# Rotary attention and softplus feed-forward on one core: the first head pair rotated through PSUM and placed by engines, the second on GpSimd, weight group 0 converted in mid loop

## Chip, cores and metric

The kernel runs on one core of one Trainium2 chip. The metric is the device time of one execution in microseconds (us). Time before the change: 745.19 us, the median of 3 runs (744.81 to 746.87).

## What is computed

Attention with rotary position embedding over 4 batches of 8 heads, 576 positions of 64 values each, and behind it a feed-forward of 2304 tokens with a softplus between two matrix products. Inputs and result are float32, the feed-forward's weights come as float64.

```python
def _attn_ref(q, k, v):                       # 4 x 8 x 576 x 64
    def rotate(x):
        x1, x2 = (x[..., :half], x[..., half:])
        return np.concatenate([x1 * cos - x2 * sin, x1 * sin + x2 * cos], axis=-1)
    q_rot, k_rot = (rotate(q), rotate(k))
    scores = scale * np.matmul(q_rot, k_rot.transpose(0, 1, 3, 2))
    scores = scores - np.max(scores, axis=-1, keepdims=True)
    attn = np.exp(scores)
    attn = attn / (np.sum(attn, axis=-1, keepdims=True) + 1e-09)
    return np.matmul(attn, v)

def _moe_ref(x, w_in, w_out):                 # 2304 x 512, 512 x 2048, 2048 x 512
    h = x @ w_in
    g = np.maximum(h, 0.0) + np.log1p(np.exp(-np.abs(h)))
    return g @ w_out
```

## The kernel before

Every matrix product is made exact enough by splitting an operand into a rounded high part and the rest (low part), both in the matmul's 32-bit format, and adding the products.

**Attention** is one loop over slots `s`; slot `s` belongs to head `s // 5` and chunk `s % 5` of 128 positions, 160 slots in all, followed by a tail. A head passes through three passes on TensorE (PE), all written into the same slot sequence. `p1` (L356) computes scores of the slot's chunk, and VectorE (DVE) takes their maximum (L358). `p2`, nine slots later (L390), computes the scores again, transposed and with the maximum subtracted as two more rows of the stacked query; ScalarE (ACT) takes the exponential twice (L396, L397) and DVE makes its low part (L404, L407). `pv`, twelve slots behind `p1` (L425), multiplies with the values. So the slots 0 to 8 hold `p1` alone, and from slot 12 on a slot holds all three.

Between `p1` and `p2` of a head lies its **shift**: GpSimd (POOL) splits the five maxima (`shift1`, tile `shl`), PE transposes them (`shift2`, L373, in slot 5h + 6 for head h), ACT rounds the result (`shr`, L375) and a DMA from ACT's queue writes it into the stacked query (`shift3`, L379, `qs<-shr`). `p2` of the head starts three slots behind the transpose and waits for that DMA.

**Rotation** goes by pairs of heads. The arrays of a pair (`raw`, one for q and one for k, 576 KB each) hold both halves in two orders, so that a rotation is: multiply with the cosine table, multiply with the sine table, add, round to the high part, subtract to the low part (`rope_steps`, L303 and L297/L300; `tab` is the table). Four DMAs per head (`stack`, L335 to L338) then place the parts into the stacked operands `qs` and `ks`, of which there are four each. Pairs 2 and on are rotated a pair ahead in the loop. Of the first pairs, pair 0 is rotated by DVE and POOL and ACT ahead of the loop, and pair 1 in slots 0 to 5.

**The feed-forward** (L203, L239) starts behind slot 168 and goes over 16 groups of the weights. A group's float64 words are turned into float32, split and stored by `conv_w`. Group 0 is loaded ahead of the loop and converted in slots 1 to 9 by ACT and DVE; group 1 is loaded in slots 92 to 134 and converted in slots 141 to 156 (`early`, `STEPS`), with its add (L146) and its low part (L151) on POOL; the others follow from slot 152 on.

**What sets the order.** A scheduler lays out the instructions; those wrapped in `pin` keep the order in which they are written, those in `chain` follow one another on their queue. Each engine, and SyncE's (SP's) DMA queue, works its instructions in that order. A warm-up of 64 matmuls on zeros (L283) fills PE until the first operands are there.

The few lines to which the steps of the prediction point:

```python
e0, e1, e2, e3 = "VVAV" if p == 0 else "VPAV" if p + i == 2 else "PPAP" if p == 1 else "PPPP"
...
if n < LAG and n % 2:
    sp = ps_v.tile([128, 2, 512], F32, tag="pv", name="sp1")
else:
    sp = ps_1.tile([128, 2, 512], F32, tag="s1", name="sp1")
```

The letters say which engine (V for DVE, P for POOL, A for ACT) does which step of a rotation. The scores of `p1` lie in a single buffer, and in slots 0 to 8 in two.

Of the kernel before, what the change touches and what calls it, by code (L numbers as in the profile page):

```python
# [30 lines left out]
FC = 2  # L31
SEG = 4
# [8 lines left out]
WARM = 64  # L41
# [11 lines left out]
def rope_attention_softplus_moe(  # L53
# [210 lines left out]
    def attention(es, es_r, es_s, tail):  # L264
# [16 lines left out]
        wp = ps_2.tile([128, 2, 512], F32, tag="s2", name="wp")  # L281
# [23 lines left out]
        def rope_steps(p):  # L305
            for i in range(2):
# [3 lines left out]
                e0, e1, e2, e3 = "VVAV" if p == 0 else "VPAV" if p + i == 2 else "PPAP" if p == 1 else "PPPP"  # L310
                yield tt(a, a, tab[:, 0, :], ALU.mult, e0)
                yield tt(b, b, tab[:, 1, :], ALU.mult, e1)
                yield tt(a, a, b, ALU.add, e0)
                yield rnd(hi[:, :S], a, e2)
                yield tt(lo[:, :S], a, b, ALU.subtract, e3)
                if i:
                    rnd(hi[:, S:], hi[:, 512:S].bitcast(F32), e2)
                    rnd(lo[:, S:], lo[:, 512:S].bitcast(F32), e2)
# [23 lines left out]
        def p1(n):
# [5 lines left out]
            if n < LAG and n % 2:  # L348
# [340 lines left out]
```

## Time and profile before

| | |
|---|---|
| median of 3 runs | 745.19 us |
| the profiled execution | 744.38 us |
| its span, first to last instruction | 742.5 us |
| PE busy | 717.1 us (97%) |
| DVE, ACT, POOL busy | 501.8, 384.3, 314.3 us |
| mean granted TensorE clock | 0.986 |
| first matmul on scores | 23.11 us |
| transposes of the shifts of heads 0, 1, 2 | 32.32, 43.40, 53.89 us |

Busy times are sums over the whole span, and the stages differ: up to some 50 us the engines wait for one another, from there to some 290 us the attention loop runs in an even beat, and behind it the feed-forward fills PE. Times in the rows are counted from the span's start; 1.88 us of the profiled execution lie outside its span.

### The profile page before, as it was taken

The page shows a single profiled execution, that of the slowest core. Times are in us where ns is not written, and L with a number is a line of the kernel's source. Part 1 is how long each engine was busy: PE and PEld are TensorE (multiplying, and loading weights), DVE is VectorE, ACT ScalarE, POOL GpSimd, SP SyncE. Part 2 cuts the span into 40 slices and gives each one's busy share as a digit, 9 for nine tenths or more (in the row PEclk, how much of TensorE's full clock was granted, in tenths as well). Part 3 has the DMA queues.
Part 4 walks back from the last instruction along what each step waited for, and adds up shares of the span by engine and source line. Part 5 has one row for each costly group of instructions (what it writes and reads, how often), then busy time and mean ns, then how long its engine had stood idle before and what let it go on. Part 6 is the DMA issues. An engine that isn't in the chain of part 4 may idle for free.

```text
span 742.5 us, 11791 instructions
## 1 busy us (share of the span) xinstructions
PE 717.1 (97%) x4288; PEld 671.2 (90%) x4288; DVE 501.8 (68%) x784; ACT 384.3 (52%) x718; POOL 314.3 (42%) x384
## 2 busy tenths in 40 slices
PE   6599999999999999999999999999999999999997
PEld 6489999999999999998999989899998989999996
DVE  7688888888788888877989989453443343344333
ACT  2267777777777777875666666232222222222221
POOL 5269999898899988884000000370400000000000
PEclk9589999999999999999999999999999999999999
DMA  7948887889898977702333333160010010001001
GB/s 235 240 133 203 202 202 199 201 219 213 216 248 215 242 186 180 198 21 85 123 114 114 129 102 115 35 203 22 22 43 0 1 44 1 0 1 43 0 1 44
DMA packets 46219, 89.05 MB, mean 120 GB/s; under 512 B 6768, under 2 KB 16304, under 8 KB 46160
## 3 DMA queue, kind: packets, MB, share of 16 engines
q1 hardware_dynamic: 43184, 83.41, 42.5%
q10 hardware_dynamic: 2976, 4.88, 1.8%
q8 instruction: 34, 0.56, 0.3%
q14 instruction: 25, 0.20, 0.1%
HBM read 48.64 MB, written 7.23 MB: 75 GB/s over the span
## 4 chain that ended last, share of the span: by engine, by line
PE 88%; DVE 5%; DMA 4%; ACT 2%; issue 1%; SPq 0%; ACTq 0%; DVEq 0%
PE hp L203 26%; PE pv L425 14%; PE oa L239 13%; PE ob L239 13%; PE sp L390 11%; PE sp L356 10%; DMA qs<-shr 2%; DVE raw L303 2%; DMA tab<-cs 1%; DMA ks<-raw 1%; DVE mx L358 1%; ACT ph L396 0%; ACT raw L297 0%; ACT sp L397 0%; DVE g L223 0%
## 5 line engine op out<-in xcount | busy, mean ns | idle before, releaser
L203 PE MATMUL hp<-x,wh 128*128 128x384 f32 x768 | 196.3, 336 | 1.2 <-DVE m L218 1.2
L358 DVE TENSOR_REDUCE mx<-sp 128x1 f32<-128x576 f32 x160 | 120.9, 755 | 55.0 <-PE sp L356 45.0
L215 ACT ACTIVATE e<-e 128x384 f32<-128x384 f32 x96 | 50.4, 525 | 198.4 <-DVE e L213 193.7
L203 PEld LDWEIGHTS hp<-x,wh 128*128 128x128 f32 x768 | 140.6, 188 | 9.8 <-DVE m L218 1.6
L356 PE MATMUL sp<-ks,qs 128*128 128x288 f32 x640 | 117.5, 308 | 13.4 <-DMA ks<-raw 9.4
L396 ACT ACTIVATE ph<-sp 128x576 fp32r<-128x576 f32 x160 | 103.8, 649 | 50.7 <-PE sp L390 50.4
L203 PE MATMUL hp<-x,wl 128*128 128x384 f32 x384 | 129.3, 337 | 0.0
L390 PE MATMUL sp<-qs,ks 128*128 128x288 f32 x640 | 114.5, 300 | 2.6 <-DVE ph L407 1.2
L356 PEld LDWEIGHTS sp<-ks,qs 128*128 128x128 f32 x640 | 96.6, 196 | 17.4 <-issue 9.6
L425 PE MATMUL pv<-ph,vs 128*64 128x288 f32 (+1 forms) x640 | 110.7, 295 | 0.0
L213 DVE TENSOR_SCALAR e<-hp 128x384 int32<-128x384 int32 x96 | 53.2, 555 | 75.4 <-PE hp L203 75.4
L397 ACT ACTIVATE sp<-sp 128x576 f32<-128x576 f32 x160 | 102.8, 642 | 0.0
L404 DVE TENSOR_TENSOR pl<-sp,ph 128x576 fp32r<-128x576 f32 x128 | 96.6, 755 | 5.6 <-ACT sp L397 4.2
L390 PEld LDWEIGHTS sp<-qs,ks 128*128 128x128 f32 x640 | 93.6, 190 | 5.5 <-DMA qs<-shr 2.4
L239 PE MATMUL oa<-wh,g 128*128 128x512 f32 x288 | 97.7, 393 | 0.0
L239 PE MATMUL ob<-wh,g 128*128 128x512 f32 x288 | 97.3, 393 | 0.0
L223 DVE TENSOR_TENSOR g<-m,g 128x384 fp32r<-128x384 f32 x96 | 56.4, 588 | 46.8 <-ACT g L220 46.8
L425 PEld LDWEIGHTS pv<-ph,vs 128*64 128x64 f32 (+1 forms) x640 | 86.7, 161 | 0.1
L303 POOL TENSOR_TENSOR raw<-raw,tab 128x576 f32<-128x576 f32 x58 | 82.6, 1446 | 9.2 <-DMA raw<-qk 9.1
L303 POOL TENSOR_TENSOR raw<-raw 128x576 f32<-128x576 f32 (+1 forms) x56 | 81.0, 1446 | 5.2 <-ACT raw L297 3.0
L218 DVE SCALAR_TENSOR_TENSOR m<-hp,e 128x384 f32<-128x384 f32 x96 | 53.5, 557 | 42.9 <-ACT e L215 41.4
L220 ACT CAST g<-m 128x384 fp32r<-128x384 f32 x96 | 49.3, 513 | 48.9 <-DVE m L218 46.0
(75 smaller groups left out, 884.9 us busy)
## 6 DMA issues: line engine op xcount, KB each, us to landing
raw<-qk SPq DMA_DIRECT2D x32, 576.0 KB
wraw<-w SPq DMA_DIRECT2D x30, 512.0 KB
ks<-raw SPq DMA_DIRECT2D x32, 320.0 KB
qs<-raw SPq DMA_DIRECT2D x32, 288.0 KB
ks<-raw SPq DMA_DIRECT2D x32, 160.0 KB
vf<-v SPq DMA_DIRECT2D x32, 160.0 KB
qs<-raw SPq DMA_DIRECT2D x32, 144.0 KB
x<-xt SPq DMA_DIRECT2D x16, 144.0 KB
```

The costliest lines, as they stand in the source:

```text
L203: pin(nc.tensor.matmul(out=hp, lhsT=a[f][:, c * 128:(c + 1) * 128], rhs=piece(j, c)[:, b, :], start=(i == 0), stop=(i == 11),))
L218: pin(nc.vector.scalar_tensor_tensor(out=m, in0=hp, scalar=0.0, in1=e, op0=ALU.max, op1=ALU.add))
L223: pin(nc.vector.tensor_tensor(out=g[:, 1, :], in0=m, in1=g[:, 0, :].bitcast(F32), op=ALU.subtract))
L239: pin(nc.tensor.matmul(out=po, lhsT=g[:, s, t * 128:(t + 1) * 128], rhs=b[f][:, 512:1024], start=(first and i == 0), stop=(last and i == 2),))
L303: pin((nc.vector if e == "V" else nc.gpsimd).tensor_tensor(out=out, in0=in0, in1=in1, op=op))
L356: pin(nc.tensor.matmul(out=sp[:, j, :HS], lhsT=q[:, i, cq], rhs=k[:, 0, ck], start=(i == 0), stop=(i == 1)))
L358: pin(nc.vector.tensor_reduce(out=mx_t[h][:, c:c + 1], in_=sp[:, :, :HS], axis=AX.XY, op=ALU.max, negate=True))
L390: pin(nc.tensor.matmul(out=sp[:, i, :HS], lhsT=k[:, j, ck], rhs=q[:, j, hs], start=(j == 0), stop=(j == 1)))
L396: pin(nc.scalar.activation(out=ph, in_=sp, func=AF.Exp, scale=D ** -0.5))
L397: pin(nc.scalar.activation(out=sp, in_=sp, func=AF.Exp, scale=D ** -0.5))
L404: pin(nc.vector.tensor_tensor(out=pl, in0=sp[:, :, :HS], in1=ph.bitcast(F32), op=ALU.subtract))
L425: pin(nc.tensor.matmul(out=pv[rows, i, :HS], lhsT=lhs, rhs=rhs[:, i, :], start=(c == 0 and j == 0), stop=(c == 4 and j == len(terms) - 1)))
```

## The change

- **Arrival.** The first q array comes in two halves on SP's queue, the table in two halves on ACT's queue, ahead of ACT's table load. The k array of pair 0, both arrays of pair 1 and both of pair 2 follow at once on SP. Nothing of weight group 0 is loaded here. The warm-up has 54 matmuls and lies in another PSUM buffer.
- **Pair 0** (`place_pair0`). ACT copies the table into PSUM (`ct`, `st`). DVE rotates q into a PSUM tile (`sq`) and k into `ct`. ACT and DVE then write high and low parts from PSUM straight into `qs` and `ks` of heads 0 and 1, across partitions where needed. The eight placing DMAs of this pair fall away.
- **Pair 1** (`rope_pair1`). All multiplications, sums and differences are POOL's, and are issued ahead of the loop and in slots 1, 2, 3 and 5; ACT rounds the high parts. Its placing DMAs follow in slots 2 (queries) and 5 (keys).
- **Pair 2** is rotated wholly by POOL (`PPPP`), as all later pairs are; before, its q array was `VPAV`.
- **Group 0** of the weights is loaded in slots 40 to 82 and converted in slots 96 to 111, in the steps of group 1, so with two adds and two subtractions on POOL.
- The memsets of two stacked queries go to DVE, those of the third and of the values' ones to POOL.

```diff
-WARM = 64
+WARM = 54
+W0 = 40
-STEPS = {141: (0,), 143: (0,), 147: (0, 1), ..., 156: (1,)}
+STEPS = {0: (0,), 2: (0,), 6: (0, 1), 7: (0,), 8: (0, 1), 10: (0,), 11: (1,), 12: (1,), 13: (1,), 15: (1,)}
+BASE = (96, 141)
...
-        wp = ps_2.tile([128, 2, 512], F32, tag="s2", name="wp")
+        wp = ps_1.tile([128, 2, 512], F32, tag="s1", name="wp")
...
+        def rope_pair1():
...
+            (qh, ql, qa, qb), (kh, kl, ka, kb) = parts
+            tt(qa, qa, tab[:, 0, :], ALU.mult, "P")
+            tt(qb, qb, tab[:, 1, :], ALU.mult, "P")
+            tt(qa, qa, qb, ALU.add, "P")
+            yield
+            rnd(qh[:, :S], qa, "A")
+            tt(ka, ka, tab[:, 0, :], ALU.mult, "P")
+            yield
+            tt(ql[:, :S], qa, qb, ALU.subtract, "P")
+            tt(kb, kb, tab[:, 1, :], ALU.mult, "P")
+            tt(ka, ka, kb, ALU.add, "P")
+            yield
+            rnd(kh[:, :S], ka, "A")
+            rnd(kh[:, S:], kh[:, 512:S].bitcast(F32), "A")
+            yield
+            tt(kl[:, :S], ka, kb, ALU.subtract, "P")
+            rnd(kl[:, S:], kl[:, 512:S].bitcast(F32), "P")
+            yield
...
+        def place_pair0():
+            ct, st = (ps_2.tile([128, 2, 512], F32, tag="s2", name=k) for k in ("ct", "st"))
+            sq = ps_v.tile([128, 2, 512], F32, tag="pv", name="sq")[:, :, :HS]
+            ct, st = ct[:, :, :HS], st[:, :, :HS]
+            pin(nc.scalar.copy(out=ct, in_=halves(tab[:, 0, :])))
+            pin(nc.scalar.copy(out=st, in_=halves(tab[:, 1, :])))
...
+            tt(qa, qa, tab[:, 0, :], ALU.mult, "V")
+            tt(qb, qb, tab[:, 1, :], ALU.mult, "V")
+            tt(sq, halves(qa), halves(qb), ALU.add, "V")
+            rnd(halves(q0[L, 0, :S]), sq[L], "A")
+            rnd(halves(q0[H, 0, :S]), sq[L], "A")
+            rnd(halves(q1[H, 0, :S]), sq[H], "A")
+            tt(halves(ka), halves(ka), ct, ALU.mult, "V")
+            tt(st, halves(kb), st, ALU.mult, "V")
+            tt(ct, halves(ka), st, ALU.add, "V")
+            sk = ct
+            rnd(halves(k0[L, 0, :S]), sk[L], "A")
+            tt(halves(q0[L, 1, :S]), sq[L], halves(q0[L, 0, :S].bitcast(F32)), ALU.subtract, "V")
+            tt(halves(k0[H, 0, :S]), sk[L], halves(k0[L, 0, :S].bitcast(F32)), ALU.subtract, "V")
+            rnd(halves(q1[L, 0, :S]), sq[H], "A")
+            yield
...
-            if n < LAG and n % 2:
+            if 1 < n < LAG and n % 2 == 0:
...
-        conv = conv_w([(0, i) for i in range(1024 // CW)], CW, pin, 2)
-        load_pair(0)
-        load_pair(1, (0,))
-        next(conv)
+        for j, e in ((1, nc.sync), (0, nc.sync)):
+            pin(e.dma_start(out=r[:, j, :S].bitcast(F32), in_=qk[0, 0, :, j]))
+            pin(nc.scalar.dma_start(out=tab[:, 1 - j, :], in_=cs[:, 1 - j, :]))
+        pin(nc.scalar.preload_act_table_set("natural_log_exp_and_others"))
+        load_pair(0, (1,))
+        load_pair(1)
+        load_pair(2)
...
-        for _ in rope_steps(0):
-            pass
-        stack(0)
-        load_pair(1, (1,))
+        place = place_pair0()
+        next(place)
+        pair1 = rope_pair1()
+        next(pair1)
...
+                if s in (1, 2, 3, 5):
+                    next(pair1)
...
-            if 0 < s < 9:
-                next(conv, None)
...
+            for f, o in enumerate((W0, WL)):
+                i, j = divmod(s - o, 6)
+                if 0 <= i < 8 and j == 0:
+                    load_p(f, i)
```

How POOL's row stands at the start, behind its memsets. Before: two steps of pair 1's q array and more, then the shift of head 0 (`shl`), pair 2, the values (`vs`), the shift of head 1.

```order
L303 TENSOR_TENSOR raw<-raw,tab 128x576 x2
L303 TENSOR_TENSOR raw<-raw 128x576 x2
L303 TENSOR_TENSOR raw<-raw,tab 128x576
L300 TENSOR_SCALAR shl<-mx 128x5
L303 TENSOR_TENSOR shl<-mx,shl 128x5
L303 TENSOR_TENSOR raw<-raw,tab 128x576
L327 TENSOR_TENSOR vs_128<-vf_126,vs_128 128x5x64
L300 TENSOR_SCALAR shl<-mx 128x5
L303 TENSOR_TENSOR shl<-mx,shl 128x5
```

The same place now.

```order
L300 TENSOR_TENSOR raw<-raw,tab 128x576 x2
L300 TENSOR_TENSOR raw<-raw 128x576
L300 TENSOR_TENSOR raw<-raw,tab 128x576
L300 TENSOR_TENSOR raw<-raw 128x576
L300 TENSOR_TENSOR raw<-raw,tab 128x576
L300 TENSOR_TENSOR raw<-raw 128x576
L297 TENSOR_SCALAR shl<-mx 128x5
L300 TENSOR_TENSOR shl<-mx,shl 128x5
L300 TENSOR_TENSOR raw<-raw 128x576
L297 TENSOR_SCALAR raw<-raw 128x64
L300 TENSOR_TENSOR raw<-raw,tab 128x576 x2
L300 TENSOR_TENSOR raw<-raw 128x576
```

Seven instructions on 128x576 now stand ahead of the shift of head 0, where there were five. Behind it, up to the shift of head 1 (the rows go on with one round-off on 128x576, the values and that shift), stand five of them, a short round-off and the values, where there was one and the values.

DVE's row at the start, from the first multiplication on. Before: rotation of pair 0, then the maxima of head 0 with steps of the conversion (`wc`) and of pair 1 between them.

```order
L303 TENSOR_TENSOR raw<-raw,tab 128x576 x2
L303 TENSOR_TENSOR raw<-raw 128x576 x2
L303 TENSOR_TENSOR raw<-raw,tab 128x576 x2
L303 TENSOR_TENSOR raw<-raw 128x576 x2
L358 TENSOR_REDUCE mx<-sp_257 128x1
L358 TENSOR_REDUCE mx<-sp_271 128x1
L138 TENSOR_SCALAR wc<-wc 128x512
L358 TENSOR_REDUCE mx<-sp_285 128x1
L303 TENSOR_TENSOR raw<-raw,tab 128x576
L143 SCALAR_TENSOR_TENSOR wc<-wraw,wc 128x512
```

And now.

```order
L300 TENSOR_TENSOR raw<-raw,tab 128x576 x2
L300 TENSOR_TENSOR sq<-raw 128x2x288
L300 TENSOR_TENSOR raw<-raw,ct 128x576
L300 TENSOR_TENSOR st<-raw,st 128x2x288
L300 TENSOR_TENSOR ct<-raw,st 128x2x288
L300 TENSOR_TENSOR qs_119<-sq,qs_119 64x576
L300 TENSOR_TENSOR ks_115<-ct,ks_115 64x576
L425 TENSOR_REDUCE mx<-sp_252 128x1
L300 TENSOR_TENSOR qs_120<-sq,qs_120 64x576
L425 TENSOR_REDUCE mx<-sp_262 128x1
L300 TENSOR_TENSOR ks_116<-ct,ks_116 64x576
L425 TENSOR_REDUCE mx<-sp_273 128x1
```

Eight instructions stand ahead of the first maximum as before, six of them with an operand or the result in PSUM; of the conversion nothing is left here.

POOL's row in mid loop, from the shift of head 20 to that of head 21 (slots 105 to 110), as it is now.

```order
L297 TENSOR_SCALAR shl<-mx 128x5
L300 TENSOR_TENSOR shl<-mx,shl 128x5
L300 TENSOR_TENSOR raw<-raw 128x576
L297 TENSOR_SCALAR raw<-raw 128x64 x2
L300 TENSOR_TENSOR raw<-raw,tab 128x576
L150 TENSOR_TENSOR wl_184<-wc,wh_183 128x512
L300 TENSOR_TENSOR raw<-raw,tab 128x576
L300 TENSOR_TENSOR raw<-raw 128x576
L145 TENSOR_TENSOR wc<-wc,wt 128x512
L582 MEMSET qs_122 2x576
L297 TENSOR_SCALAR raw<-raw 128x576
L387 TENSOR_TENSOR vs_125<-vf_123,vs_125 128x5x64
```

Two instructions of the conversion (`wl`, `wc`) stand between two shifts that had none; one more stands ahead of the first of these shifts and one behind the second.

## Rows read from the trace of the kernel before

**Rows 1.** Timeline, PE at the start: start, us, engine, line, operation, [wait <-releaser].

```profile
23.11 4.44 PE L356 MATMUL sp<-ks,qs 128*128 128x288 f32 x16 [9.37 <-DMA ks<-raw]
...
32.32 0.28 PE L373 MATMUL sp<-identr,shl 128*10 128x128 f32 x1 [1.71 <-POOL shl L303]
...
38.94 1.09 PE L390 MATMUL sp<-qs,ks 128*128 128x288 f32 x3 [0.80 <-DMA qs<-shr]
39.83 1.28 PE L356 MATMUL sp<-ks,qs 128*128 128x288 f32 x4
...
42.86 0.70 PE L390 MATMUL sp<-qs,ks 128*128 128x288 f32 x4
43.40 0.22 PE L373 MATMUL sp<-identr,shl 128*10 128x128 f32 x1
...
53.89 0.22 PE L373 MATMUL sp<-identr,shl 128*10 128x128 f32 x1
```

**Rows 2.** Windows: stretch, its length, busy us by engine, granted clock, DMA share, GB/s.

```profile
20.00:25.00 5.00, 1.89 (x8) 1.92 (x8) 0.55 (x1) 0.00 (x0) 0.00 (x0) 0.50 1.02 281
...
35.00:40.00 5.00, 3.62 (x13) 3.16 (x14) 5.00 (x9) 1.86 (x5) 0.88 (x1) 0.50 0.92 220
...
50.00:60.00 10.00, 10.00 (x78) 9.92 (x76) 8.22 (x12) 7.21 (x14) 8.72 (x13) 1.00 0.64 140
```

**Rows 3.** The chain that ended last, in order of time: start, us, what.

```profile
1.48 4.96 DMA tab<-cs
...
18.30 4.56 DMA ks<-raw
...
35.81 3.09 DMA qs<-shr
```

**Rows 4.** Timeline, ACT, POOL and DVE on pairs 0 and 1 ahead of the loop.

```profile
6.54 1.43 DVE L303 TENSOR_TENSOR raw<-raw,tab 128x576 f32<-128x576 f32 x2 [0.62 <-DMA tab<-cs]
...
8.79 0.68 ACT L297 CAST raw<-raw 128x576 fp32r<-128x576 f32 x1 [6.77 <-DVE raw L303]
...
10.04 3.43 POOL L303 TENSOR_TENSOR raw<-raw,tab 128x576 f32<-128x576 f32 x2 [3.46 <-DMA raw<-qk]
10.18 3.91 DVE L303 TENSOR_TENSOR raw<-raw,tab 128x576 f32<-128x576 f32 x2
```

**Rows 5.** Page, costliest groups: line, engine, operation, count | busy us, mean ns.

```profile
L404 DVE TENSOR_TENSOR pl<-sp,ph 128x576 fp32r<-128x576 f32 x128 | 96.6, 755 | 5.6 <-ACT sp L397 4.2
```

**Rows 6.** Groups of POOL's instructions, 60 to 280 us, shapes kept apart.

```profile
L303 POOL TENSOR_TENSOR raw<-raw,tab 128x576 f32<-128x576 f32 x48 | 67.9, 1437 | 0.1
...
L327 POOL TENSOR_TENSOR vs<-vf,vs 128x320 fp32r<-128x320 f32 x24 | 21.0, 877 | 0.0
L300 POOL TENSOR_SCALAR raw<-raw 128x576 fp32r<-128x576 f32 x23 | 15.5, 675 | 2.1
L509 POOL MEMSET qs<- 2x576 f32 x24 | 13.7, 573 | 1.4
L300 POOL TENSOR_SCALAR raw<-raw 128x64 fp32r<-128x64 f32 x24 | 5.4, 247 | 0.0
```

**Rows 7.** Timeline, POOL at the shifts of heads 3 and 4.

```profile
61.15 0.20 POOL L300 TENSOR_SCALAR shl<-mx 128x5 fp32r<-128x5 f32 x1 [0.37 <-DVE mx L358]
61.43 0.20 POOL L303 TENSOR_TENSOR shl<-mx,shl 128x5 fp32r<-128x5 f32 x1
...
70.31 0.20 POOL L300 TENSOR_SCALAR shl<-mx 128x5 fp32r<-128x5 f32 x1 [0.74 <-DVE mx L358]
```

**Rows 8.** Timeline, PE's weight load for the transpose of head 3's shift.

```profile
62.93 0.09 PEld L373 LDWEIGHTS sp<-identr,shl 128*10 128x10 f32 x1
```

**Rows 9.** Timeline, POOL on group 1 of the weights.

```profile
299.01 1.29 POOL L146 TENSOR_TENSOR wc<-wc,wt 128x512 int32<-128x512 int32 x1 [0.63 <-DVE wc L143]
```

**Rows 10.** Windows, a stretch in which group 1 is converted.

```profile
300.00:310.00 10.00, 9.47 (x70) 8.96 (x69) 9.14 (x13) 7.65 (x15) 7.91 (x10) 1.00 0.92 271
```

**Rows 11.** Timeline, PE behind a late shift DMA.

```profile
132.95 0.66 PE L390 MATMUL sp<-qs,ks 128*128 128x288 f32 x3 [0.36 <-DMA qs<-shr]
```

More of the change, by code (lines that the diff above doesn't have):

```diff
@@ L289, in load_pair @@
                 r = raw_p.tile([128, 2, SP], F32R, tag="raw", name="raw")
-                (pin if p < 2 else chain)(nc.sync.dma_start(out=r[:, :, :S].bitcast(F32), in_=qk[p, i]))
+                (pin if p < 3 else chain)(nc.sync.dma_start(out=r[:, :, :S].bitcast(F32), in_=qk[p, i]))
                 hl_t[p, i] = r
-                if p == 0 and i == 0:
-                    nc.sync.dma_start(out=tab, in_=cs)
         def rnd(out, in_, e):
@@ L309, in rope_steps @@
                 a, b = lo[:, :S].bitcast(F32), hi[:, :S].bitcast(F32)
[L310 to L315, printed above, removed]
[L316 to L318 removed]
+                yield tt(a, a, tab[:, 0, :], ALU.mult, "P")
@@ L512, in attention @@
             if s < NSLOT:
+                if s < 2:
+                    next(place)
+                if s in (1, 2, 3, 5):
+                    next(pair1)
+                if s == 2:
+                    next(place)
+                    for i in (2, 3):
+                        stack_q(i, chain)
+                if s == 5:
+                    for i in (2, 3):
+                        stack_k(i, chain)
                 next(rope, None)
-                if s < 5:
-                    next(rope, None)
                 if s % 10 == 5:
@@ L533, in attention @@
                 recip(n3 // (5 * NH) - 1)
-            if 0 < s < 9:
-                next(conv, None)
-                if s % 2:
-                    next(conv, None)
-            if s == 9:
-                for _ in conv:
-                    pass
             tail(s)
@@ L604, in tail, with load_p @@
                 convert()
[L606 to L610 removed]
+        kind, dt = ("wc", I32) if w.dtype == F32 else ("wraw", I64)
+        pre = {}
+        early = {}
+        def load_p(f, n):
             i, j = divmod(n, 4)
             m = slice(j * CW // 4, (j + 1) * CW // 4)
[L613 to L614 removed]
+            if j == 0:
+                if f:
+                    pre[f, i] = mp["wr"].tile([128, CW], dt, tag="wr", name="wr")
+                else:
+                    pre[f, i] = cv_p.tile([128, CW], dt, tag=kind, name=kind, bufs=3)
+            chain(nc.sync.dma_start(out=pre[f, i].bitcast(w.dtype)[:, m],
+                                    in_=w[f, :, i * CW + m.start:i * CW + m.stop]))
         cuts = [(c, 0, S) for c in range(4)] + [(c, S, 2 * T) for c in range(4)] + [(c, 2 * T, 3 * T) for c in range(4)]
```

88 lines of the change are left out of this document (53 added, 35 removed).

## The prediction

> **What bounds the kernel now.** I read the windows first. From 50 us on PE is busy without a gap at a granted clock of 1.00, the full 2.4 GHz, whereas between 20 and 25 us and between 35 and 40 us it works 1.89 and 3.62 us of 5 at a clock of 0.50, which is 1.2 GHz [rows 2]. So behind some 50 us only PE's own work counts, and an edit there costs time only if it makes PE wait; the 50 us ahead of that are a chain of waits, and whatever shortens it moves everything behind it forward one for one. The chain in order of time and PE's timeline show what it is made of. The first scores start at 23.11 us, behind the landing of the last key part [rows 1, 3]. The transpose of head 0's shift follows at 32.32, having waited 1.71 us for POOL; `p2` of head 0 at 38.94, behind the shift's DMA; the transposes of heads 1 and 2 stand at 43.40 and 53.89 us [rows 1]. I use these five moments as milestones: what the milestone of head 2 gains, the end gains, less what mid loop loses.
>
> **The start, step by step.** *Arrival.* Table and q are the first two arrays of 576 KB, and the later one, the table, is there at 1.48 + 4.96 = 6.44 us [rows 3]; the fourth array, q of pair 1, lets POOL start at 10.04 [rows 4]. That is 1.8 us an array, so that k of pair 0 (third) comes at about 8.2 and k of pair 1 (now fifth, no longer behind the weights) at about 11.8. The halves on two queues carry the same bytes; I count on the second halves at 6.44 as now, and nothing for the split.
>
> *Pair 0.* A DVE multiplication takes 1.43/2 = 0.72 us [rows 4], and one that reads PSUM 0.755 [rows 5]. After 6.44: the second product 0.72 and the sum 0.755, so 7.9. k waits until 8.2: three steps of 0.755 end at 10.5. One ACT rounding, 0.68 [rows 4], ends at 11.2, one DVE difference at about 12.0: there `p1` can begin, 11 us ahead of 23.11. The eight placing DMAs leave, of which the last alone took 4.56 us [rows 3], and so does the slow pass of DVE: its two key products took 3.91 us, 1.95 each, while POOL's two beside them took 3.43, 1.72 each [rows 4], against 0.72 and 1.437 undisturbed [rows 4, 6].
>
> This last point rests on pair 0's route through PSUM. The rows show that two SBUF operands on DVE beside POOL slow both, and that DVE's PSUM reader at 0.755 runs while POOL holds 1.437 all through the loop [rows 5, 6]. The Trainium skill, "SBUF — State Buffer", "Who interferes with whom", says so as a rule: DVE contends with a GpSimd instruction that reads SBUF when it has two SBUF inputs, and not with at most one. The trace agrees. By that rule pair 0 would pay nothing for POOL's work on pair 1.
>
> *Pair 1, the new bound.* That gain doesn't reach the end in full, because POOL now has a row of its own. From 10.04 on seven instructions of 1.437 [rows 6] stand ahead of head 0's shift: 10.04 + 10.06 = 20.1, and with the two shift instructions (0.48 from 61.15 to 61.63 [rows 7]) 20.6. The fourth of the seven needs k of pair 1 at 11.8 and starts at 14.4, so doesn't wait; ACT's rounding lies beside it. The five `p1` of head 0, at 0.70 at full clock or 1.28 at half [rows 1], each with a maximum of about 0.755 behind it, partly in turn on one buffer, end between 18 and 20: just covered. The transpose takes 0.28 [rows 1], ACT's cast at most 0.68, the shift's DMA 3.09 [rows 3]: `p2` of head 0 at about 24.5 instead of 38.94, a gain of 14.4. The placing of pair 1's keys runs beside that: its last part leaves at 22.5 and, at 3 to 4.6 us a DMA [rows 3], is there between 25.5 and 27, where PE reaches it at about 26.5.
>
> Up to head 1's shift POOL has: 0.68 of ACT's rounding to wait for (to 20.8), then 1.437, 0.247, three times 1.437, 0.675, 0.877 and 0.48 [rows 6, 7]: 28.9. PE from 24.5 took 43.40 - 38.94 = 4.46 for that piece [rows 1]: 29.0. Both say 28.9, a gain of 14.5. Up to head 2's shift POOL has four times 1.437, 0.573, 0.675, 0.877 and 0.48, 8.35 us: 37.2. PE took 10.49 there [rows 1], with waits for DVE's steps of conversion and rotation, which are gone; its full beat of a head is, by two shifts, 70.31 - 61.15 = 9.16 [rows 7]. So 38.1, a gain of 53.89 - 38.1 = **15.8 us**.
>
> The bounds: POOL's twelve instructions up to head 1's shift could run at 1.72 [rows 4] instead of 1.437, 3.4 us more; PE could stay at half clock from 24.5 to head 1's shift, five groups of 1.28 instead of 0.70, of which POOL hides all but 2 us; the two add up only in part. On the other side k and q could come 0.7 us sooner, with no weights in the queues, and the PE beat up to head 2 is a `pv` short: 1 us together. I take 15.8, and keep 11.5 and 16.8 as ends.
>
> **Mid loop.** Group 0 adds four instructions on POOL, 1.29 us each [rows 9], in the intervals of the shifts of heads 19 to 22: one, two, one. POOL's interval of a head takes 9.16 less its wait of 0.74, 8.42 [rows 7], and 0.49 more in every second one for two round-offs of 0.247 [rows 6]; PE's beat is 9.16. A shift may come 62.93 - 61.63 = 1.30 us late before PE waits [rows 7, 8]. First interval 8.42 + 1.37 (with the gap between instructions) = 9.79: 0.63 late, covered. Second 8.91 + 2.74 = 11.65: 0.63 + 2.49 = 3.12 late, PE waits 1.82. Third 9.79: 1.30 + 0.63, PE waits 0.63 again. From then on POOL catches up. That is **2.4 us**, a cover that is used up, not absent. ACT's and DVE's steps of one group sit in PE's way too: where group 1 is converted, PE works 9.47 of 10 us [rows 10], so 0.5. The eight loads of 128 KB each share queues with the shift's DMA, which once held PE for 0.36 [rows 11]; I take one or two such waits, 0.5. Mid loop together 3.4, between 1 (POOL's lag absorbed) and 6 (POOL waits for its inputs besides, as the 0.63 before its add [rows 9], in all four places).
>
> **Priced at nothing.** Memsets moved to POOL end before 10.04, where POOL waited 3.46 us [rows 4]. Warm-up: PE has nothing else. The feed-forward is untouched and starts with the same queue of conversions.
>
> **The sum.** The profiled execution took 744.38 us, 742.5 of it span. 744.38 - 15.8 + 3.4 = 732.0. The median of the three runs lies 0.81 above this execution, so 732.8; I say **733**.
>
> **The rivals.** *The head start is eaten by a slow start* (0.18): POOL's rate of 1.72 or the half clock, with the late ends above: gain 11.5, time 737. For it speaks that PE's short bursts between 35 and 40 us ran at 0.50 [rows 2], and `p1` in the new start is again bursts; against it that the new bursts follow the warm-up without the gap of 9.37 us [rows 1]. The Trainium skill, "TensorE: Matmul & The Clock Gate", "A second HAM failure mode: psum-queue depth-cycling", tells that small idle times between groups of matmuls while PSUM is cycled make the clock swing. By the rows this would put the time at 737.
>
> *Mid loop costs more* (0.08): waits for inputs on POOL and the lag passing on to the placing of the next pair: 6 to 8 instead of 3.4, so 736 to 738. For it speaks that POOL has 8.42 to 8.91 of 9.16 filled; against it that group 1 cost little, though without rotations beside it.
>
> *POOL's lag is absorbed* (0.10): mid loop 1, start 16.8: 729.4.
>
> *Slower than before* (0.03): the shift's DMA. If the changed phase between loads and shifts made every one of the 27 later heads wait, each 0.45 us would cost 12.2 and the gain be gone; with 0.6 each, 16.2, the time is 749. For it: a transfer did come late [rows 11]; against it: PE stands for it in one row of the loop.
>
> *No change* (0.02): the placing by engines across partitions, of which no row shows a price, takes as long as the eight DMAs did, and `p1` of head 0 comes at 23 again: 744 to 747.
>
> **How the numbers follow.** The forecast has 0.59, from 730 to 735.5; the slow start 0.18, dear mid loop 0.08, absorbed lag 0.10, slower 0.03, no change 0.02. A range of 729 to 738 leaves out the last two cases and the far ends of the others, some 0.15. A measurement of this kernel tells 0.3% (2.2 us) from no change: faster 0.95, same 0.02, slower 0.03.
>
> **What would show it.** First `p1` at 12, the transposes of heads 0, 1 and 2 at 20.6, 28.9 and 38, POOL without a gap from 10 us to the shift of head 0, and its instructions there at 1.44; PE waiting for `shl` at heads 21 and 22 alone, 2.4 us in all, and an unchanged length from there to the end. Wrong would be a first wait on something other than POOL between 12 and 38 us, a granted clock of 0.50 past 30 us, or a PE that waits in heads that convert nothing.

## The result and the profile after

The changed kernel takes 734.43 us in the median of 6 runs (733.85 to 741.76), the kernel before in the same comparison 745.41 (744.81 to 746.87). The ratio is 0.9867, 95% interval 0.9828 to 0.9905: faster by 1.3%. The profiled execution took 733.85 us, its span is 732.0. The prediction was 733 (729 to 738) from a sum of 732.0 for that execution. One run of the six, 741.76 us, stands apart; no profile shows it.

PE's timeline of the changed kernel at the start answers to [rows 1] (start us, us, engine, line, operation, in brackets the wait and what ended it; L423 is `p1`, L440 the transpose of a shift, L457 `p2`):

```profile
12.41 0.76 PE L423 MATMUL sp<-ks,qs 128*128 128x288 f32 x4 [1.34 <-DVE ks L300]
...
22.47 0.28 PE L440 MATMUL sp<-identr,shl 128*10 128x128 f32 x1 [3.70 <-POOL shl L300]
...
26.67 0.66 PE L457 MATMUL sp<-qs,ks 128*128 128x288 f32 x3 [0.51 <-DMA qs<-shr]
...
28.72 0.80 PE L423 MATMUL sp<-ks,qs 128*128 128x288 f32 x4 [0.28 <-DVE mx L425]
...
30.82 0.23 PE L440 MATMUL sp<-identr,shl 128*10 128x128 f32 x1 [0.51 <-POOL shl L300]
...
40.00 0.22 PE L440 MATMUL sp<-identr,shl 128*10 128x128 f32 x1
```

The first scores start at 12.41 instead of 23.11 us, the wait of 9.37 us for the placing DMAs is gone, and the longest wait is now for POOL, as the prediction said: 3.70 us ahead of head 0's shift. `p2` of head 0 goes on at 26.67 after its wait for the shift's DMA, the moment for which 24.5 was predicted. The transpose of head 2 stands at 40.00 instead of 53.89: a gain of 13.89, where 15.8 was predicted. POOL and ACT between 14 and 23 us (L300 are POOL's two-operand steps, L294 ACT's roundings) show where most of the difference arose:

```profile
14.39 1.41 POOL L300 TENSOR_TENSOR raw<-raw,tab 128x576 f32<-128x576 f32 x1
...
16.44 0.64 ACT L294 CAST ks<-ct 64x576 fp32r<-64x576 f32 x1 [3.51 <-DVE ks L300]
16.98 0.67 ACT L294 CAST raw<-raw 128x576 fp32r<-128x576 f32 x1
...
17.73 1.41 POOL L300 TENSOR_TENSOR raw<-raw 128x576 fp32r<-128x576 f32 x1 [1.92 <-ACT raw L294]
...
21.94 0.20 POOL L297 TENSOR_SCALAR shl<-mx 128x5 fp32r<-128x5 f32 x1
```

POOL's steps take 1.41, the uncontended price, but there is a hole of 1.92 us: its difference needs ACT's rounding of pair 1 (16.98), and ACT had idled 3.51 us in front of another cast, the second copy of head 1's keys, which waited for DVE. The rounding's operand had been ready since 14.4.

The windows (stretch, its length, busy us by engine, then granted clock, DMA share, GB/s) answer to [rows 2]:

```profile
15.00:20.00 5.00, 2.94 (x16) 2.06 (x15) 4.28 (x6) 3.40 (x10) 3.08 (x3) 1.00 0.19 53
20.00:25.00 5.00, 2.53 (x10) 2.29 (x11) 0.94 (x2) 1.61 (x4) 4.42 (x7) 0.75 0.78 179
25.00:30.00 5.00, 4.21 (x23) 3.46 (x23) 3.24 (x5) 2.32 (x5) 4.83 (x5) 0.91 0.94 220
```

The stretches at 0.50 are gone; from 30 us on the clock is 1.00. In mid loop the timeline shows the cost of group 0 (L137 and L142 are DVE's conversion steps, L145 and L150 POOL's):

```profile
194.13 1.11 DVE L137 TENSOR_SCALAR wraw<-wc 128x512 int32<-128x512 int32 x1
...
196.09 0.80 PE L423 MATMUL sp<-ks,qs 128*128 128x288 f32 x4 [0.35 <-DVE mx L425]
...
203.99 0.80 PE L423 MATMUL sp<-ks,qs 128*128 128x288 f32 x4 [0.38 <-DVE mx L425]
...
211.93 1.93 DVE L142 SCALAR_TENSOR_TENSOR wc<-wraw 128x512 int32<-128x512 int32 x1
...
214.59 0.80 PE L423 MATMUL sp<-ks,qs 128*128 128x288 f32 x4 [0.90 <-DVE mx L425]
...
219.11 0.23 PE L440 MATMUL sp<-identr,shl 128*10 128x128 f32 x1 [0.56 <-POOL shl L300]
...
228.69 0.23 PE L440 MATMUL sp<-identr,shl 128*10 128x128 f32 x1 [0.25 <-POOL shl L300]
```

PE waits for shifts at heads 21 and 22, as predicted, but only 0.81 us in all; three waits, 1.63 us together, are for DVE's maxima, which stand behind conversion steps. The four intervals between transposes that end at heads 19 to 22 take 9.79, 10.01, 11.32 and 9.58, against 9.17, 9.16, 9.18 and 9.15 before: **4.04 us more**.

The difference of the two executions, 744.38 - 733.85 = 10.53, by the transposes: 13.89 up to head 2; 0.52 more by head 15 (before lost 0.61 in the interval ahead of head 11, where PE waited 0.36 for a shift's DMA [rows 11]; after didn't); -0.63 in heads 16 to 18; -4.04 in heads 19 to 22; -0.33 by head 31; and 1.12 regained after the last transpose, 0.66 of it in one wait of the feed-forward for DVE, 1.20 us before and 0.54 after; the rest was not followed up.

### The profile page after: what moved, and what is told of

It is laid out like the page before. It is cut to its first block, busy times and chain, and to the rows that moved or that the text cites. A ratio compares the mean times of both kernels' runs of the same rounds, so it can differ in the third digit from the quotient of the medians.

```text
span 732.0 us, 11761 instructions
## 1 busy us (share of the span) xinstructions
PE 712.4 (97%) x4278; PEld 665.3 (91%) x4278; DVE 491.6 (67%) x771; ACT 389.2 (53%) x729; POOL 329.2 (45%) x401
## 4 chain that ended last, share of the span: by engine, by line
PE 62%; POOL 4%; DMA 2%; DVE 2%; ACT 1%; issue 1%; SPq 0%; POOLq 0%; ACTq 0%
PE hp L202 27%; PE oa L238 13%; PE ob L238 13%; PE pv L492 4%; PE sp L457 3%; POOL raw L300 3%; PE sp L423 2%; DMA qs<-shr 1%; DMA raw<-qk 1%; DMA x<-rd 1%; POOL raw L297 0%; POOL wc L145 0%; POOL vs L387 0%; POOL wl L150 0%; DMA vf<-v 0%
## 5 line engine op out<-in xcount | busy, mean ns | idle before, releaser
L423 PE MATMUL sp<-ks,qs 128*128 128x288 f32 x640 | 114.9, 303 | 5.2 <-DVE mx L425 3.7
L457 PE MATMUL sp<-qs,ks 128*128 128x288 f32 x640 | 113.8, 299 | 2.9 <-DMA qs<-shr 1.6
L423 PEld LDWEIGHTS sp<-ks,qs 128*128 128x128 f32 x640 | 93.9, 191 | 9.4 <-DVE mx L425 6.1
L457 PEld LDWEIGHTS sp<-qs,ks 128*128 128x128 f32 x640 | 92.8, 189 | 6.3 <-DMA qs<-shr 2.6
L300 POOL TENSOR_TENSOR raw<-raw 128x576 f32<-128x576 f32 (+1 forms) x60 | 86.0, 1433 | 4.6 <-ACT raw L294 2.3
L300 POOL TENSOR_TENSOR raw<-raw,tab 128x576 f32<-128x576 f32 x60 | 84.7, 1431 | 1.5 <-DMA raw<-qk 1.5
```

The costliest lines, as they stand in the source:

```text
L300: pin((nc.vector if e == "V" else nc.gpsimd).tensor_tensor(out=out, in0=in0, in1=in1, op=op))
L423: pin(nc.tensor.matmul(out=sp[:, j, :HS], lhsT=q[:, i, cq], rhs=k[:, 0, ck], start=(i == 0), stop=(i == 1)))
L457: pin(nc.tensor.matmul(out=sp[:, i, :HS], lhsT=k[:, j, ck], rhs=q[:, j, hs], start=(j == 0), stop=(j == 1)))
```

## Experiments

For each run: transposes of heads 0 and 2; the interval that ends at head 18; what the four intervals ending at heads 19 to 22 take beyond 4 x 9.17; PE's waits for the shift's DMA from 45 to 320 us (a run's own "waits" view); the time.

| kernel | head 0 | head 2 | to 18 | 19 to 22 | DMA waits | us (runs) |
|---|---|---|---|---|---|---|
| before | 32.32 | 53.89 | 9.46 | 0.0 | 0.4 | 745.41 (6) |
| after | 22.47 | 40.00 | 9.93 | 4.0 | 1.1 | 734.43 (6) |
| act_order | 20.16 | 38.01 | 10.31 | 4.1 | 1.0 | 732.14 (4) |
| sbuf_keys | 22.16 | 39.74 | 10.43 | 4.0 | 1.7 | 734.27 (1) |
| no_conv | 22.09 | 40.46 | 10.68 | 0.0 | 2.4 | 733.25 (1) |
| dve_conv | 22.12 | 40.25 | 10.52 | 3.8 | 2.7 | 736.2 (1) |
| before_mid | 29.92 | 52.74 | 9.16 | 5.0 | none | 747.02 (1) |
| start_conv | 25.11 | 45.02 | 9.27 | 1.1 | none | 735.87 (1) |
| warm16 | 23.12 | 41.25 | 12.87 | 3.3 | 2.2 | 736.79 (1) |
| spread | 20.60 | 38.48 | 11.99 | 1.8 | 3.5 | 733.16 (5) |
| no_pool | 22.29 | 40.16 | 10.16 | 2.3 | 1.7 | 733.84 (1) |
| pool_only | 22.48 | 40.84 | 10.38 | 1.6 | 2.4 | 734.90 (1) |
| early_loads | 20.21 | 38.21 | 9.75 | 4.1 | 1.2 | 733.17 (4) |
| act_pair1 | 21.49 | 38.89 | 10.00 | 4.1 | 3.2 | 734.93 (4) |

Beside them the kernel before took 746.51 us (act_order, sbuf_keys, no_conv, dve_conv), 747.16 (before_mid, start_conv, warm16, spread) and 744.73 (the last four), and single executions of it ran from 743.10 to 750.01, so a single time says little. The arguments below rest on the transposes, of which each kernel has one profile; in the five kernels that start alike (after, no_conv, dve_conv, no_pool, pool_only) those of heads 0 and 2 spread over 0.4 and 0.8 us.

**act_order: what made the hole of 1.92 us.** The second placing step comes behind pair 1's first rounding.

```
-                if s < 2:
+                if s == 0:
                     next(place)
                 if s in (1, 2, 3, 5):
                     next(pair1)
+                if s == 1:
+                    next(place)
```

> The changed kernel with one edit: ACT rounds the high part of pair 1's q array before it writes the second copy of head 1's key high part, not after. Theory (POOL's row of pair 1 sets the start, and the 1.92 us in which POOL waited for ACT at 17.7 us is an accident of ACT's order): POOL's wait falls to under 0.3 us, the transposes of the shifts of heads 0, 1, 2 come 1.5 to 2.0 us earlier than 22.47, 30.82, 40.00, and the whole by as much: ratio to the kernel before 0.984 to 0.985, 732 to 733 us. Rival (the scores and maxima of head 0 or the placing DMAs of pair 1 set the start anyway): transposes of heads 1 and 2 move by less than 0.5 us and the time stays at 734.

POOL's row of this kernel:

```profile
14.02 1.42 POOL L300 TENSOR_TENSOR raw<-raw,tab 128x576 f32<-128x576 f32 x1
15.40 1.41 POOL L300 TENSOR_TENSOR raw<-raw 128x576 fp32r<-128x576 f32 x1
16.77 1.41 POOL L300 TENSOR_TENSOR raw<-raw,tab 128x576 f32<-128x576 f32 x1
18.26 1.40 POOL L300 TENSOR_TENSOR raw<-raw 128x576 f32<-128x576 f32 x1
19.63 0.20 POOL L297 TENSOR_SCALAR shl<-mx 128x5 fp32r<-128x5 f32 x1
```

No hole; the shifts of heads 0, 1 and 2 come 2.31, 2.27 and 1.99 us sooner. Of this, 0.39 is chance: POOL's first product started at 9.78 instead of 10.17, when its array came. The 1.92 of the hole is the edit's, so ACT's order was its cause. The ratio is 0.9806 (0.9774 to 0.9838), the lowest median here.

**sbuf_keys: does the way of the keys' tables through PSUM matter?** `k` of pair 0 is multiplied with the tables in SBUF.

```
-            tt(halves(ka), halves(ka), ct, ALU.mult, "V")
-            tt(st, halves(kb), st, ALU.mult, "V")
+            tt(ka, ka, tab[:, 0, :], ALU.mult, "V")
+            tt(kb, kb, tab[:, 1, :], ALU.mult, "V")
-            tt(ct, halves(ka), st, ALU.add, "V")
+            tt(ct, halves(ka), halves(kb), ALU.add, "V")
```

> The changed kernel, with the two key products and the first operand of the sum of pair 0 in SBUF (the table is read from SBUF, only the sum goes to PSUM). Theory (two SBUF operands on DVE and POOL's reads slow one another, and the route through PSUM is what avoids it): those of DVE's three key steps that fall behind POOL's start at 10.17 us take up to 1.9 us instead of 0.76, POOL's step beside them 1.7 instead of 1.4; as only the sum and perhaps the second product overlap, first scores come 0.5 to 1.5 us later than 12.41, and as POOL's row sets the start, the shifts of heads 0 to 2 move by 0.3 to 0.8 us. Rival (no contention here): all within 0.2 us.

The transposes of heads 0 to 2 came 0.26 to 0.32 us sooner, as POOL's start did (9.85 instead of 10.17). DVE's two products ran from 8.20 to 9.63, and POOL began at 9.85, so little was left to contend: POOL's first two steps, beside DVE's sum, took 1.64 each instead of 1.39, and that was made up by the hole behind them, 1.43 instead of 1.92. For `k` the way through PSUM brought nothing in this start; the slow pass of [rows 4] was cured by the order, at least as far as this run shows: DVE's key products end at 9.63, before POOL starts, while before the change they ran from 10.18, beside POOL's steps on pair 1 (pair 0 had no steps on POOL there either; its letters are `VVAV`).

**no_conv and dve_conv: what mid loop costs.** The first leaves group 0's conversion out (`for i in STEPS.get(s - BASE[f], ()) if f else ():`; DVE writes zeros for its weights), the second does POOL's four steps on DVE (`nc.gpsimd if f else nc.vector`).

> The changed kernel with the conversion of weight group 0 left out (its loads in slots 40 to 82 stay; high and low parts of that group are zeros written by DVE in eight pieces of about 0.3 us, so the feed-forward lacks that group). Theory: the heads 19 to 22, whose shifts took 9.79, 10.01, 11.32 and 9.58 us apart, go back to 9.2 each, 4.0 us in all; a wait for the shift's DMA in one to three heads stays. Span 728 us. Rival (the loads, or the state that the loop is in, cost it): those intervals keep more than 2 us of their excess, span 730 or more.

> The changed kernel with the two additions and the two differences of group 0's conversion on DVE instead of POOL. Theory (POOL's lag is the larger part of the 4.0 us in heads 19 to 22): POOL keeps up with the shifts, and the excess falls to 1 to 2 us, made of ACT's and DVE's extra steps in PE's way; span 729 to 730. Rival (ACT's and DVE's steps in PE's way are what costs): four more steps on DVE, of some 0.7 us each, raise the excess to 5 us or more, span 733.

Without the conversion heads 19 to 22 are back at 9.17, so the 4.0 us are all the conversion's. On DVE they cost 3.8 instead of 4.0: my expectation of 1 to 2 failed, and so did the rival's 5 or more. In heads 19 to 22 no wait for a shift was left, but the waits for DVE's maxima grew to 1.97 us (0.34, 0.42, 0.96 and 0.25). Both runs also lost where nothing had been edited: 1.3 us ahead of head 5, where PE waited for the shift's DMA (as in the two runs that follow). So the spans I expected, 728 and 729 to 730, did not come: 731.5 and 734.4.

**no_pool and pool_only: which engine's steps make the 4.0.** The first leaves out POOL's two steps for each half (its edit below; the difference is left out in the same way), the second keeps them alone, on zeros.

```
-                keep(e.tensor_tensor(out=wf, in0=wf, in1=t3, op=ALU.add))
+                if f or not spread:
+                    keep(e.tensor_tensor(out=wf, in0=wf, in1=t3, op=ALU.add))
...
```

> The changed kernel without the four steps of group 0's conversion on POOL (the addition and the difference; the low part of group 0's weights is set to zero instead); the steps on ACT and DVE stay. Theory (the steps on DVE and ACT stand in PE's way, POOL's lag is only what the trace names): of the 4.0 us that heads 19 to 22 take beyond 9.17 each, 2.0 to 3.2 stay. Rival (the prediction's own split: POOL's lag 2.4, the other steps 0.5): 0.4 to 1.2 us stay.

> The changed kernel with only the four POOL steps of group 0's conversion (on zeros; the steps on ACT and DVE and so group 0's true weights are left out). Theory: POOL's lag alone costs 0.8 to 2 us in heads 19 to 22. The prediction's split as the rival: 2.4 us, with PE's waits for the shift in heads 21 and 22 alone.

PE's transposes of heads 18 to 22 (five rows each), first in no_pool, then in pool_only:

```profile
188.98 0.22 PE L442 MATMUL sp<-identr,shl 128*10 128x128 f32 x1
...
198.76 0.22 PE L442 MATMUL sp<-identr,shl 128*10 128x128 f32 x1
...
208.78 0.22 PE L442 MATMUL sp<-identr,shl 128*10 128x128 f32 x1
...
218.80 0.22 PE L442 MATMUL sp<-identr,shl 128*10 128x128 f32 x1
...
227.99 0.22 PE L442 MATMUL sp<-identr,shl 128*10 128x128 f32 x1
```

```profile
190.23 0.22 PE L447 MATMUL sp<-identr,shl 128*10 128x128 f32 x1
...
199.40 0.22 PE L447 MATMUL sp<-identr,shl 128*10 128x128 f32 x1
...
208.56 0.22 PE L447 MATMUL sp<-identr,shl 128*10 128x128 f32 x1
...
218.94 0.23 PE L447 MATMUL sp<-identr,shl 128*10 128x128 f32 x1 [1.04 <-POOL shl L307]
...
228.55 0.23 PE L447 MATMUL sp<-identr,shl 128*10 128x128 f32 x1 [0.30 <-POOL shl L307]
```

ACT's and DVE's steps alone cost 0.61, 0.85, 0.85 and 0.02: 2.3 us, without one wait for a shift. POOL's steps alone cost nothing, nothing, 1.21 and 0.44: 1.6 us, of which 1.34 are named waits for shifts. The two add up to the 4.0 of the whole, and head by head too: 0.61, 0.85, 2.06 and 0.46 against 0.62, 0.84, 2.15 and 0.41 in the changed kernel. Which part of the 2.3 is ACT's and which DVE's, no run tells.

**spread: the steps spread over more heads** (with act_order's edit): one POOL step in every second head.

```
+SPREAD = {91: (0,), 93: (0,), 97: (0,), 98: (0,), 99: (0,), 108: (0,),
+          101: (1,), 103: (1,), 117: (1,), 118: (1,), 119: (1,), 128: (1,)}
...
-                for i in STEPS.get(s - BASE[f], ()):
+                for i in (STEPS.get(s - BASE[f], ()) if f else SPREAD.get(s, ())):
```

> The changed kernel with two edits: the second copy of pair 0's keys is put behind pair 1's first rounding on ACT (as in the run before that did this alone, 732.1 us), and group 0's conversion is spread in mid loop, one POOL step in every second head instead of one, two and one in three heads on end. Theory (POOL's lag is most of the 4.0 us that heads 19 to 22 take beyond 9.17 each): POOL has 0.25 to 0.74 us of spare in a head and a lag of 1.30 is free, so single steps of 1.37 are absorbed; what stays are ACT's and DVE's steps in PE's way, 1 to 2 us over all the heads from 16 to 30. Time 729.5 to 730.5. Rival (DVE's and ACT's steps are the cost, wherever they stand, as the run with the steps on DVE suggests): the sum over those heads stays at 3 to 4 us and the time at 732.

The waits for shifts went: in the intervals of heads 21 and 25, where a POOL step stands alone, PE lost 0.05 us and nothing. The intervals ahead of heads 19, 20 and 23, with steps of ACT and DVE, took 0.64, 1.09 and 0.77 more, 2.5 us; ahead of head 18, where such steps stand too, a long wait for a DMA hides their cost. The 0.82 ahead of head 24 is another thing; no step of the conversion stands there, and PE waited for a shift's DMA:

```profile
236.86 0.22 PE L442 MATMUL sp<-identr,shl 128*10 128x128 f32 x1
...
242.92 0.66 PE L459 MATMUL sp<-qs,ks 128*128 128x288 f32 x3 [0.61 <-DMA qs<-shr]
...
246.85 0.22 PE L442 MATMUL sp<-identr,shl 128*10 128x128 f32 x1
```

So the theory is right about POOL's part, 1.6 us of the 4.0, which is gone, and the rival about the rest: the steps of ACT and DVE cost 0.6 to 1.1 a place wherever they stand. The time I expected, 729.5 to 730.5, did not come. In the profiled execution that wait ahead of head 18 took 2.61 us; ratio 0.9802 (0.9784 to 0.9819), no better than act_order.

**early_loads: the late shift DMA** (with act_order's edit): `W0 = 32` for 40.

> The changed kernel with the second copy of pair 0's keys behind pair 1's first rounding on ACT (732.1 us alone, ratio 0.9806) and with group 0's eight weight loads started 8 slots, some 15 us, sooner, so that none is in the queue beside the two arrays of 576 KB when head 18's shift leaves. Theory (that collision makes the wait of 0.57 to 2.61 us for head 18's shift, which changes from run to run): the interval of head 18 falls from 10.3 (9.9 to 12.9 in the runs so far) to 9.2 to 9.7, and the time to 731.0 to 731.8, ratio about 0.979. Rival (the two arrays alone make it, or the loads collide in another head): head 18 stays above 9.9 or another head pays, 732 or more.

Head 18 paid less (9.75 instead of 10.31 in act_order), but the intervals ahead of heads 11 and 12 took 9.99 and 9.54 instead of 9.19 and 9.24. The rival again: PE waited 0.65 and 0.18 us for the shift's DMA there. Ratio 0.9851 (0.9831 to 0.9871). What such a late DMA stands beside is seen in the chain of waits of spread (start, us, what):

```profile
176.87 0.23 ACT ph L465
177.10 7.37 DMA qs<-shr
184.47 0.04 issue
184.51 0.67 PE sp L459 x3
```

5 KB need 7.37 us here, where [rows 3] have 3.09. Between 175.0 and 178.2 the queue was given two arrays of 576 KB, 160 KB of values, 128 KB of weights and two blocks of 144 KB; from 176 to 184 us the DMA engines were 95 to 97% busy.

**before_mid and start_conv: each half of the change alone.** The first is the kernel before with group 0's conversion in mid loop, the second the changed kernel with it in the start; the lines that the first takes out and the second puts back:

```
...
             if 0 < s < 9:
                 next(conv, None)
                 if s % 2:
                     next(conv, None)
...
```

> The kernel before with one part of the change alone: group 0 is loaded and converted in mid loop, while pairs 0 and 1 are rotated and placed as before. Theory (the start is set by the rotation and placing of the pairs, not by the conversion): the first scores still wait for the last placed key part, 20 to 23 us (23.11 before); the conversion's steps between the first two full heads go, so that the transpose of head 2's shift comes 2 to 4 us earlier (50 to 52 instead of 53.89); mid loop loses the 4 us that it lost in the changed kernel. Together 743 to 747 us. Rival (the conversion's leaving is what freed the start): the transpose of head 2 comes 8 us or more earlier, at 46 or before, and the time is 740 or less.

> The changed kernel, but group 0 is loaded and converted in the start as before, with pairs 0 and 1 handled as the change has them. Theory: heads 19 to 22 keep the plain 9.17 us (4.0 us less); in the start the weight blocks delay pair 1's keys by some 2 to 4 us and the conversion's four POOL steps of about 1.3 us stand in POOL's row, which sets the shifts there, so that the transpose of head 2 comes 3 to 6 us later than 40.00, at 43 to 46: 733 to 736 us in all. Rival (the start has room for it, since DVE and ACT idle there): head 2 at 41 or before and the time 730 to 731, that is, moving the conversion was a loss.

In before_mid the transpose of head 2 gained 1.15 us (I expected 2 to 4) and mid loop lost 5.0: no gain in time. In start_conv head 2 lost 5.0 and mid loop got back 2.9; 735.87 in all. That 1.1 us stayed in heads 19 and 20, where this kernel converts nothing, I had not expected; what makes them is open. PE and POOL of that run show who was in the way in the start:

```profile
21.11 1.33 PE L423 MATMUL sp<-ks,qs 128*128 128x288 f32 x4 [5.14 <-DVE mx L425]
...
24.09 0.68 POOL L297 TENSOR_SCALAR shl<-mx 128x5 fp32r<-128x5 f32 x1 [2.58 <-DVE mx L425]
```

The maxima wait behind DVE's conversion steps, of which the first, at 18.69, had itself waited 2.79 us for ACT's part of the conversion. So moving the conversion pays only together with the new handling of pairs 0 and 1 (5.0 us at the start for 2.9 in mid loop): where the placing DMAs bound the start, most of it was covered.

**warm16: PE's clock in the start.** `WARM = 16` for 54.

> The changed kernel with 16 instead of 54 warm-up matmuls, so that the first scores may run at half clock. Theory (POOL's row sets the start, PE's clock up to 25 us is covered): the five score tiles take up to 1.28 instead of 0.70 us each, yet the transposes of heads 0 and 1 move by less than 0.7 us (22.47 and 30.82), head 2's by less than 1 us (40.00), and the time stays within 733.5 to 735.5. Rival (the slow start of the prediction: PE's clock decides): the transpose of head 2 at 41.5 to 44 and 735.5 to 738 us.

PE ran at 0.50 from 10 to 25 us, `p1` took 1.30 instead of 0.76 for four matmuls, and the transposes of heads 0, 1 and 2 came 0.65, 0.65 and 1.25 us later, although POOL had started 0.44 us sooner (9.73 instead of 10.17). POOL's hole grew from 1.92 to 3.02: the late scores held up DVE's last placing step, and with it ACT's cast and the rounding behind that. So the half clock cost some 1.7 us up to head 2, 1.1 of it by way of the hole; the rest is covered by POOL. The time, 736.79, is outside what I expected, but 2.9 us more than in the changed kernel were lost ahead of head 18, where PE waited 1.96 us for the shift's DMA.

**act_pair1: two of pair 1's steps on DVE** (with act_order's edit):

```
-            tt(ka, ka, tab[:, 0, :], ALU.mult, "P")
+            tt(ka, ka, tab[:, 0, :], ALU.mult, "V")
...
-            tt(ka, ka, kb, ALU.add, "P")
+            tt(ka, ka, kb, ALU.add, "V")
```

> The changed kernel with the second copy of pair 0's keys behind pair 1's first rounding, and besides with two of pair 1's seven steps ahead of head 0's shift (the cosine product and the sum of its keys) on DVE instead of POOL. Theory (POOL's row alone sets head 0's shift; PE's last maximum of head 0 ends at 19.4): the shift's transpose moves from 20.16 to 18.7 to 19.9, less than the 2.8 us that POOL saves, since DVE's two steps delay its maxima and run beside POOL with two SBUF operands, at up to 1.95 us each and with POOL at 1.72; head 2's transpose at 36.8 to 37.8 (38.01) and the time 730.8 to 731.9. Rival (contention and DVE's queue take all back): head 0's shift at 20.2 to 22 and 732 to 733.5.

```profile
15.57 1.59 DVE L300 TENSOR_TENSOR raw<-raw,tab 128x576 f32<-128x576 f32 x1
...
16.50 1.91 POOL L300 TENSOR_TENSOR raw<-raw,tab 128x576 f32<-128x576 f32 x1
...
18.80 0.80 PE L423 MATMUL sp<-ks,qs 128*128 128x288 f32 x4 [2.42 <-DVE mx L425]
...
20.95 0.20 POOL L297 TENSOR_SCALAR shl<-mx 128x5 fp32r<-128x5 f32 x1 [2.54 <-DVE mx L425]
```

The rival holds: DVE's step took 1.59 and POOL's beside it 1.91, the maxima came late, and POOL, with less to do, waited 2.54 us for them. Head 0's shift is 1.33 later than in act_order, 0.28 of it by POOL's later start (10.06 instead of 9.78). The ratio is 0.9869 (0.9831 to 0.9908), the time above what I or the rival had given; 3.2 us of this execution are waits for the shift's DMA. Taking these two steps from POOL's row does not shorten the start; other ways were not tried.

## Why the prediction was right, and where it missed

*Arrival, first scores.* Predicted 12.0, measured 12.41; the 0.4 is `k`, which came at 8.59 instead of 8.2. The placing by engines costs what its model rows gave (0.755 and 0.68) or a little less: 0.74 to 0.76 on DVE, 0.63 on ACT.

*Pair 1 on POOL: the step that was mis-sized.* "The fourth of the seven ... doesn't wait; ACT's rounding lies beside it" took a free ACT for granted. The rounding was ready to start at 14.4 and ran at 16.98, since a cast that depended on DVE's last placing step stood ahead of it. That is 1.92 us, and all of the miss at the transposes: 20.6, 28.9 and 38.1 were predicted, 22.47, 30.82 and 40.00 measured, 20.16, 28.55 and 38.01 in act_order. I had priced each engine's row by its own durations, and not read ACT's order for what its front instruction waits for.

*Mid loop: too small, and by the wrong split.* Conversion 2.4 (POOL's lag) + 0.5 (ACT and DVE) was predicted, 1.6 + 2.3 measured. POOL's lag, put at 1.82 and 0.63 for heads 21 and 22, cost 1.21 and 0.44 in pool_only. ACT's and DVE's steps were under-sized more than fourfold: the 0.53 that PE lacked in one stretch of 10 us [rows 10] was taken for the whole, and is near what one place costs (0.61 to 0.85 in no_pool), of which there are three. One of DVE's steps was slow besides (L142 took 1.93 us beside POOL's product, 0.63 elsewhere), but the sum of the parts leaves only 0.09 for that. The trace of the kernel before had a nearer price. Its intervals up to the transposes of heads 28, 29 and 30 hold the conversion of group 1, beside the last rotation steps and the splitting of the feed-forward's tokens on POOL (the transposes of heads 27 to 30):

```profile
284.29 0.22 PE L373 MATMUL sp<-identr,shl 128*10 128x128 f32 x1
...
294.10 0.22 PE L373 MATMUL sp<-identr,shl 128*10 128x128 f32 x1
...
303.99 0.23 PE L373 MATMUL sp<-identr,shl 128*10 128x128 f32 x1
...
313.59 0.23 PE L373 MATMUL sp<-identr,shl 128*10 128x128 f32 x1
```

They take 9.81, 9.89 and 9.60, which is 1.8 us over 3 x 9.17, where the one stretch gave 0.5. The DMAs were put at 0.5; heads 16 to 18 and 26 took 1.1 more than before.

*What balanced it.* Start 1.9 short and mid loop 5.0 (4.04 + 0.63 + 0.33) instead of 3.4 would have given 735.5. The 0.52 up to head 15 and the 1.12 behind the last transpose, neither in the sum, brought it to 733.85. That the time is 1.4 us from the prediction is in part luck.

*The signs named ahead.* Of those for the forecast, first scores at 12 came, POOL's instructions at 1.41 too. The row without a gap did not, nor 2.4 us of waits for shifts. Two of the signs of being wrong came as well: PE's first waits from 12 us on were for DVE (1.34 us up to 12.41, 0.85 up to 14.02), and PE waited for the shift's DMA in heads that convert nothing (0.29, 0.57 and 0.28). The first belongs to the hole: DVE's last placing step, for which ACT's cast waited, stands behind the first two maxima, and these behind PE's scores. The second cost about 1 us.

*Two slips in the bounds.* Of the twelve instructions priced at 1.72 one is a round-off of 0.675, so 3.4 should be 3.1; and a mid loop of 6 to 8 gives 735.4 to 737.4 by the sum, not 736 to 738. Neither moves the forecast.

*The rivals.* The slow start's causes did not both come: POOL ran at 1.41, not 1.72. The half clock did come, in some executions only: 0.53 and 0.50 in no_conv from 20 to 30 us, where the granted clock of after is 0.75 and 0.91. From the transpose of head 0 to that of head 2 no_conv took 18.37 us and after 17.53, so 0.84 more, and with the first scores at 0.50 too (warm16) the price was some 1.7. That is under half of the 4 us that I gave the rival. The Trainium skill ("TensorE: Matmul & The Clock Gate", "A second HAM failure mode: psum-queue depth-cycling") tells of a kernel whose clock swings as PE idles briefly between groups of matmuls while PSUM is cycled; the traces here show that the clock dropped, not from what. The dear mid loop came halfway (5.0 between 3.4 and 6 to 8). The shift's DMA, my way to slower, is real, but strikes none to three heads of 30: 1.1 us in after, up to 3.5 in the others.

*Not settled.* Executions of one kernel differ by 1 us (act_order) to 8 us (the changed kernel), and profiles differ by DMA waits and by the clock before 30 us; which of them makes which run was not shown. So act_order's edit is shown for the start: head 0's transpose comes at 20.16 to 20.60 in the three kernels with it that leave pair 1's steps alone, and at 22.09 to 22.48 in the five that start alike without it. But the gain in time over the changed kernel, 0.9806 against 0.9867, has overlapping intervals. No run takes the parts of the new start (arrival in halves, placing by engines, pair 1 on POOL) singly; that the placing made the gain is read from the wait of 9.37 us for the placing DMAs [rows 1], which is gone.

## What to carry to other kernels

When steps move to other engines, price the order as well as the durations: for each instruction on the new path look up what stands ahead of it on its engine and what that one waits for; here a single cast that stood too early cost 1.92 us. Work that is moved from a start into a full loop costs what it takes from the engines between the bound engine's instructions (here 2.3 of 4.0 us on ACT and DVE), and spreading it does not lower that (2.5 in spread, where only POOL's 1.6 went). Leaving out one engine's part at a time, as no_pool and pool_only did, gave parts that added up. Where the same work already stands in another stretch of the loop, price it by the intervals there, not by PE's busy share in one window.

## What the runs showed of the hardware

DVE's integer steps took longer beside POOL's two-operand steps: L137, with one SBUF operand, 1.11 us in the changed kernel's mid loop and 0.43 in the feed-forward, where POOL was quiet; L142, with two, 1.93 and 0.63. The Trainium skill, "SBUF — State Buffer", "Who interferes with whom", states that a DVE instruction with two SBUF inputs contends with a GpSimd instruction that reads SBUF, and not with one that only writes it. The trace agrees: beside a memset of POOL, L142 took 0.68 in no_pool. The same section of the Trainium skill names L137's operation, `tensor_scalar`, among those that can contend with GpSimd through a two-port mode; the 1.11 fits that, but no run shows the mode.

A DMA of 5 KB on its own queue took 7.37 us when 1.7 MB had been issued on another in the 2 us ahead of it and the 1 us behind, and its lateness changed from one execution to the next of nearly the same kernel: PE's wait ahead of head 18 was 0.57, 1.96 and 2.61 us in after, warm16 and spread.
